# Subtracting the row maximum of two groups of local attention scores inside PSUM, with one exponential for a whole bank

## The chip, the cores and the metric

The program runs on one core of a Trainium2 chip. The metric is the device time of one execution, in microseconds (us). Before the change the median of three runs is 656.81 us, with 656.26 the lowest and 657.3 the highest. A core has a matrix engine (TensorE, PE in the profile), a vector engine (VectorE, DVE), an activation engine (ScalarE, ACT), GpSimd (POOL) and SyncE (SP), which issues the DMAs here. TensorE writes its results to PSUM; everything else lies in SBUF.

## The reference, cut to what matters

The input is q, k and v of 4 batches, 8 heads, 576 positions and 64 features. Each batch goes through an attention with two parts, whose outputs are added:

```
out_d     = softmax attention over q, k, v averaged over groups of 4 positions, repeated 4 times
scores    = q @ k.T / 8, with -1e9 where |i - j| >= 4
scores    = scores - max(scores, axis=-1)
attn      = exp(scores);  attn = attn / (sum(attn) + 1e-9)
out_local = attn @ v
x         = out_d + out_local
```

Then a mixer follows (Fourier transforms over positions and features, their real part added to x, a layer norm, a feed-forward layer of 512 to 2048 to 512), and a gated layer with a short causal convolution and two products of 512 by 512. The change concerns the local attention, and only that of batch 0.

## The kernel before

The local scores are made in windows: 58 query positions see 64 key positions. Two windows make a pair on the 128 partitions, and the five pairs form three groups: pair 0, pairs 1 and 2, pairs 3 and 4. For a group of two pairs the scores of 4 heads stand in one PSUM bank of 128 x 512 (2 pairs x 4 heads x 64 keys), and those of the other 4 heads in another. In the code `par` is the bank, `z` the pair and `a` the head in it.

Batch 0 has steps of its own, in `chain0`; the other batches use `attn_steps`. For each group g of batch 0 there are these steps: `S` (`score`, L1612 and L1622) puts the mask into the bank with a product of identity and band and adds the products of q and k; `M` (`score_max`, L1635) takes the maximum of each row of 64 on VectorE; `X` (`score_exp`, L1640 and L1645) multiplies the maxima by -1/8 and takes the exponential, one ScalarE instruction for each pair and head, since the maximum goes in as a bias of one number a partition, and each gives its row sum through ScalarE's accumulator; `N` (`score_norm`) divides; `T` (`turn`, L1659) transposes on TensorE; `V` (`value`, L1671 and L1683) multiplies with v, on top of the coarse attention's output `base`; `B` (`value_add`, L1693) copies into `X`.

The coarse attention runs beside it for four pairs of heads a: `s` scores (L1705), `m` maxima (L1712), `x` exponentials (L1721), `n` diagonal of reciprocals, `t` (L1738) and `v` (L1747). `q` and `k` pool positions for it (L1697), and `p` pools v on TensorE (L1761). Meanwhile `w` steps decode the eight blocks of the first weight matrix on VectorE, in three passes each (the first at L618, the others at L519), and further steps decode the second matrix. When X is complete, VectorE folds it (`f`, L1790), ScalarE and VectorE split it into two 16-bit parts (`h`, `l`), TensorE mirrors it (`R`, L1826 and L1827) and makes the Fourier products (`e`, L1816; then `Q`, `I`), VectorE adds the results back, and `O` (L1900) centres the input of the first of 12 units of 192 positions. From there a main stage runs, nearly all of it matrix products (the first are L1280).

The order on every engine is written out by hand: `ORDER` lists for each engine the steps by number, with the instructions of a step after a point (so "46.2" is instruction 2 of step 46). In the numbering 19, 26 and 35 are `S0`, `S1`, `S2`; 20, 30, 41 the maxima; 24, 36, 46 are `X0`, `X1`, `X2`; 32, 52, 70 `N0` to `N2`; 107 is the first fold and 163 the centring `O`. Of the decoding 79 is the third pass of block 3, 143 that of block 4, 129 that of block 5, 84 the first pass of block 7; 131 converts the convolution weights; 167 to 169 decode blocks of the second matrix. Step 0 has the memset of `ones`, step 185 the windows of v for batch 1, 183 the scale of W1, 195 a pooling of batch 1.

Of the kernel before, what the change touches and what calls it, by code (L numbers as in the profile page):

```python
# [9 lines left out]
F32 = mybir.dt.float32  # L10
# [3 lines left out]
AF = mybir.ActivationFunctionType  # L14
ALU = mybir.AluOpType
# [13 lines left out]
SCALE = 0.125  # L29
# [25 lines left out]
0 2 1 4 3 5.1 5.0 11 13 7 6 14 16.0 9 8 195.1 10 16.1 12 15.0-1 15.4 15.2 199 195.0 15.3 122 123.0 119.2 201 15.5  # L55
123.1 16.2 119.3 200 119.0 185.0 202 119.1 170 204 203 172.0 206 171 172.1 205 173 174 219.1 185.1 219.0 185.2 237.1
237.0 238.1 238.0 317.1 292 293 296.1 296.0 270 316.1 297 279 316.0 317.0 367.1 318.0 332 367.0 318.1 368.0 318.2
368.1 378.2 378.0 349 378.1 369.1 369.0 370.0 353 370.1 387.0 378.4 378.3 387.1-2 488.1 436.1 394.0-2 387.3-4 397.0-2
398.1 394.4 435.1 386 398.0 394.3 398.2 402.0-2 397.3-4 488.0 418 435.0 409.0-1 402.3-4 409.2 436.0 437.0 415.1 415.0
415.2 409.3-4 415.3 422.0-1 415.4 422.2-4 494.1 494.0 437.1 475 491.0 437.2 462 491.1 505.0 492 505.1 493 520 530 540  # L60
583.1 551 528.1 528.0 503 583.0 562.0 528.2 563 562.1 548 544 569 576.1 576.0 591 598.1 598.0 581 605.0 613.0 605.1
613.1 621.1 621.0 628 635 643.1 643.0 611 622 651 657.1 657.0 672.0 665.1 665.0 672.1 679 641 680 670 684.1 684.0 703
706 707
""",
    "gpsimd": """
5.0 0.0 5.1 136 195.1 0.1 139 137.1 137.0 195.0 294.0 183.0-1 183.3 183.2 193 219.1 219.0 225.0 237.1 225.1-2 121
195.2 237.0 237.2 225.3 219.2 238.1 238.0 238.2 267.1 267.0 275 277 282 280 283.1 283.0 285.0 294.1-3 291.0-1 294.4
291.2-6 298.0 291.7-8 298.1-2 286.1 298.3 286.0 285.1 347.0-1 326 347.2-3 333 367.1 367.0 345 367.2 368.0-1 369.1
# [21 lines left out]
344.1 347.1 333.2 345.1 355.2 355.0 355.3 355.1 356.3 333.3 359.3 356.0 462.1-2 347.2 356.1 388 356.2 359.0 347.3-6  # L90
# [297 lines left out]
S_K = -11.75  # L388
# [1734 lines left out]
```

## Time and profile before

| what | value |
|---|---|
| median of 3 runs | 656.81 us (656.26 to 657.3) |
| the profiled execution's own time | 656.03 us |
| its span, first to last instruction | 654.2 us |
| instructions in the span | 20464 |
| mean granted TensorE clock | 0.991 of full |

The profile is of one execution, so sums of its instructions are to be set against 656.03 us; 1.8 us of that lie outside the span. The median of the runs is 0.8 us above it. A busy TensorE in this profile is not TensorE at its peak: matmuls are pipelined, their ends are modelled, and the granted clock can be half. Idle time of an engine is listed with what ended it.

### The profile page before, as it was taken

Reading aid. Unit: us, or ns where it says so; the run is one execution under the profiler, and the core shown is the slowest. Engines: PE = TensorE matmul, PEld = TensorE weight load, DVE = VectorE, ACT = ScalarE, POOL = GpSimd, SP = SyncE. Lnnn points to the kernel's source line nnn. Section 1 sums busy time; section 2 is a strip of 40 time slices with the busy share of each in tenths; the row PEclk is TensorE's granted clock in tenths of the full one; section 3 lists DMA queues with packets and bytes.
Section 4 is the critical chain, followed back from the end, with each engine's and each line's share of the span. In section 5 each row is a group of like instructions: output and inputs, shape, how many; then the busy total and the mean of one; then the engine's idle time right before and its main releaser. Section 6 shows DMA issues by size and latency. Waiting matters only on the chain.

```text
span 654.2 us, 20464 instructions
## 1 busy us (share of the span) xinstructions
PE 644.7 (99%) x8658; PEld 576.2 (88%) x8659; DVE 524.6 (80%) x1142; ACT 357.2 (55%) x1057; POOL 109.8 (17%) x162
## 2 busy tenths in 40 slices
PE   9999999999999999999999999999999999999997
PEld 4768899999998897998998888997899989998995
DVE  3899899899897978688999858996878868686564
ACT  2787577888535666777454788544232333314223
POOL 0000131420211802710311154031100200200000
PEclk9969999999999999999999999999999999999999
DMA  9995493222343011344363372263424233225301
GB/s 295 416 360 145 166 324 134 74 75 98 103 141 117 18 59 44 111 130 115 121 208 123 101 246 99 78 220 100 151 94 152 98 130 117 112 67 184 123 3 49
DMA packets 44302, 89.98 MB, mean 138 GB/s; under 512 B 3391, under 2 KB 24895, under 8 KB 43186
## 3 DMA queue, kind: packets, MB, share of 16 engines
q1 hardware_dynamic: 44210, 88.67, 40.6%
q8 instruction: 68, 1.11, 0.7%
q14 instruction: 24, 0.20, 0.1%
HBM read 73.77 MB, written 16.65 MB: 138 GB/s over the span
## 4 chain that ended last, share of the span: by engine, by line
PE 93%; DVE 3%; ACT 2%; POOL 1%; issue 0%; DVEq 0%; POOLq 0%
PE pc L1386 25%; PE ph L1316 12%; PE ph L1337 8%; PE out L1507 7%; PE val L1491 6%; PE p L1337 6%; PE pc L1291 3%; PE ph L1280 3%; PE ab L1067 1%; PE dO L876 1%; PE po L1761 1%; PE po L1601 1%; PE sc L954 1%; PE po L999 1%; PE st L1151 1%; PE pq L1090 1%
## 5 line engine op out<-in xcount | busy, mean ns | idle before, releaser
L1386 PE MATMUL pc<-hh,W 128*128 128x192 f16 x1232 | 170.2, 246 | 0.0
L1386 PEld LDWEIGHTS <-W 128*128 128x128 f16 x1848 | 152.4, 98 | 4.5 <-issue 2.8
L1386 PE MATMUL pc<-hl,W 128*128 128x192 f16 x616 | 129.5, 246 | 0.0
L1316 PE MATMUL ph<-u,W 128*128 128x192 f16 x960 | 94.3, 246 | 0.7 <-ACT u L1196 0.4
L1316 PEld LDWEIGHTS <-W 128*128 128x128 f16 x960 | 80.1, 98 | 3.0 <-issue 0.9
L1337 PEld LDWEIGHTS <-W 128*128 128x128 f16 x1632 | 77.9, 98 | 2.2 <-issue 0.2
L519 DVE SCALAR_TENSOR_TENSOR W<-X,cw,W 128x192 f32<-128x192 f32 x160 | 63.2, 427 | 0.4 <-ACT W L1454 0.2
L1337 PE MATMUL ph<-u,W 128*128 128x96 f16 x960 | 62.8, 206 | 0.0
L1349 ACT ACTIVATE hh<-r 128x384 f16<-128x384 f32 x48 | 23.7, 517 | 70.8 <-DVE r L525 60.0
L1491 PE MATMUL val<-yy,W 128*128 128x192 f16 x576 | 58.2, 246 | 0.2 <-DVE W L519 0.2
L1491 PEld LDWEIGHTS <-W 128*128 128x128 f16 x576 | 47.6, 98 | 2.4 <-issue 1.2
L1337 PE MATMUL p<-u,W 128*128 128x96 f16 x672 | 48.0, 206 | 0.0
L1507 PE MATMUL out<-W,gh 128*128 128x512 f16 x144 | 46.0, 379 | 0.0
L525 DVE TENSOR_TENSOR r<-ph,r 128x384 f32<-128x384 f32 (+1 forms) x48 | 21.8, 455 | 26.3 <-PE ph L1337 21.1
L840 ACT ACTIVATE dP<-dS,dmx 128x64 f32<-128x64 f32 x120 | 36.2, 331 | 1.5 <-PE dPT L859 1.2
L525 DVE TENSOR_TENSOR r<-p,r 128x192 f32<-128x192 f32 (+1 forms) x72 | 27.7, 418 | 6.5 <-PE p L1337 4.9
L519 DVE SCALAR_TENSOR_TENSOR hl<-r,hh 128x384 f16<-128x384 f32 x48 | 26.7, 576 | 7.8 <-ACT hh L1349 7.7
L1320 ACT ACTIVATE hh<-ph 128x384 f16<-128x384 f32 x40 | 19.4, 487 | 20.7 <-PE ph L1316 17.3
L519 DVE SCALAR_TENSOR_TENSOR W<-W,W 128x1024 int32<-128x1024 int32 x24 | 29.3, 1230 | 0.1
L1507 PE MATMUL out<-W,gl 128*128 128x512 f16 x72 | 27.3, 379 | 0.0
L519 DVE SCALAR_TENSOR_TENSOR hl<-ph,hh 128x384 f16<-128x384 f32 x40 | 21.8, 551 | 6.8 <-ACT hh L1320 3.8
L840 ACT ACTIVATION_READ_ACCUMULATOR dP<-dS,dmx 128x1 f32 x120 | 27.0, 225 | 0.0
(308 smaller groups left out, 1429.7 us busy)
## 6 DMA issues: line engine op xcount, KB each, us to landing
W<-sums SPq DMA_DIRECT2D x32, 512.0 KB
W<-in_moe_w_ch_dram SPq DMA_DIRECT2D x12, 1024.0 KB
sm<-sums SPq DMA_DIRECT2D x16, 512.0 KB
out_dram<-osb SPq DMA_DIRECT2D x17, 256.0 KB
vw<-in_vw_dram SPq DMA_DIRECT2D x8, 512.0 KB
w1f<-W SPq DMA_DIRECT2D x8, 512.0 KB
sums<-so SPq DMA_DIRECT2D x16, 256.0 KB
v<-in_vp_dram SPq DMA_DIRECT2D x24, 144.0 KB
```

The lines of the kernel that those rows point to most:

```text
L519: return eng.scalar_tensor_tensor(out=out, in0=in0, scalar=scalar, in1=in1, op0=op0, op1=op1)
L525: return eng.tensor_tensor(out=out, in0=a, in1=b, op=ALU.add)
L840: A.activation(out=s_[:, z, a], in_=pss[par][:, z, a], func=AF.Exp, scale=SCALE, bias=mx[:, par, z, a:a + 1], accum_out=su[:, par, z, a:a ...
L1280: T.matmul(out=ps[:, e], lhsT=W[AT[kc * 2 + m // 8] + 1][:, o:o + 128], rhs=u()[:, kc, :], start=(kc == 0), stop=(kc == 3))
L1291: T.matmul(out=c["ps"][m // 2][:, m % 2], lhsT=W[9 + g][:, o:o + 128], rhs=hs[g // 2][:, g % 2, e, :], start=(kk == 0 and m % 2 == 0), sto ...
L1316: T.matmul(out=ps[:, e], lhsT=w1_ap(pw, kc, 2 * g + e), rhs=uh[px][:, kc, :], start=(t == 0), stop=(t == 11))
L1320: A.activation(out=h_, in_=ps, func=AF.Relu)
L1337: T.matmul(out=out[:, e * HT:e * HT + HT], lhsT=w(pw, kc, e), rhs=b_[x](px, kc), start=(kc, pw, px) == (0, 0, 0), stop=(kc, pw, px) == (1, ...
L1349: A.activation(out=h[0], in_=x, func=AF.Relu)
L1386: T.matmul(out=ps[m // 2][:, m % 2], lhsT=w2_ap(pw, kk, m), rhs=x[px][:, e], start=(kk == 0 and (pw, px) == (0, 0) and m % 2 == 0), stop=( ...
L1491: T.matmul(out=ps[:, e], lhsT=wv_ap(pw, kc, 2 * mh + e), rhs=m_["y"][px][:, kc, :], start=(t == 0), stop=(t == 11))
L1507: T.matmul(out=ps, lhsT=(gh, gl)[px][:, kc, t * 128:(t + 1) * 128], rhs=wo_ap(pw, kc), start=(n == 0), stop=(n == 11))
```

## The change

For groups 1 and 2 of batch 0 (`ONE_EXP`) the maxima are multiplied by -1 in place of -1/8. Then TensorE makes the scores a second time into the same banks, mask and products of q and k, and adds a product of the fp32 identity with the negated maxima, each spread over its 64 columns. The bank then holds the scores less their maxima, and one exponential with the scale 1/8 takes all 512 columns. Its row sums are made by VectorE from the result. Group 0 is left as it was, and so are the other batches. The written order is a new one for the first part on every engine, up to about step 245; behind that it is the same.

```diff
+ONE_EXP = (1, 2)
...
-                T.matmul(out=ps, lhsT=eyeb, rhs=m, start=True, stop=False)
                 pss.append(ps)
+            S_["ps", g] = pss
+            score_sum(g, m)
+            S_["m", g] = m
+
+        def score_sum(g, m, neg=None):
+            prs, pss = GROUPS[g], S_["ps", g]
+            n = len(prs)
+            for par in range(2):
+                T.matmul(out=pss[par], lhsT=eyeb, rhs=m, start=True, stop=False)
+                if neg is not None:
+                    T.matmul(out=pss[par], lhsT=eye, rhs=neg[:, par].unsqueeze(3).to_broadcast([P, n, 4, WK]),
+                             start=False, stop=False)
             for z, pr in enumerate(prs):
...
         def score_exp(g):
             n = len(GROUPS[g])
             su[g] = tiny.tile([P, 2, n, 4], F32, tag="dsu", name="dsu")
-            A.activation(out=mx[g], in_=mx[g], func=AF.Copy, scale=-SCALE)
+            A.activation(out=mx[g], in_=mx[g], func=AF.Copy, scale=-1.0 if g in ONE_EXP else -SCALE)
+            if g in ONE_EXP:
+                score_sum(g, S_["m", g], mx[g])
+                for par in range(2):
+                    s_ = S_[g, par] = sp.tile([P, n, 4, WK], F32, tag="S", name="dP", bufs=NS)
+                    A.activation(out=s_, in_=S_["ps", g][par], func=AF.Exp, scale=SCALE)
+                    V.tensor_reduce(out=su[g][:, par], in_=s_, axis=AX.X, op=ALU.add)
+                return
```

The first part of the order, for VectorE up to the centring (step 163), for ScalarE up to the last copy into X (103), and the head of SP's:

```diff
     "sync": """
-0 2 1 4 3 5.1 5.0 11 13 7 6 14 16.0 9 8 195.1 10 16.1 12 15.0-1 15.4 15.2 199 195.0 15.3 122 123.0 119.2 201 15.5
+0 1 2 3 4 5.0 11 14 6 5.1 7 9 13 8 185.0 10 12 15.0 16.1 15.2-5 15.1 195.0 123.0 122.0 201 195.1 16.2 16.0 119.1 123.1
...
     "vector": """
-0 30 20 21 18 32 25 28 41.1 41.0 131.0 48.0 38.0 48.1 38.1 48.2 23 48.3 27 131.1 54.0-1 31 34 54.2 58.0 54.3 65 42 59
-58.1 71.0-1 77.0 71.3 71.2 77.1 86 75 55 85 56 130 63 52.0-1 81.0 52.2-3 132 60 68 73 70.0 83 70.1-2 81.1 70.3 140 67
-81.2 129 81.3-5 107.1 107.0 113.0 109.1 109.0 81.6 110 113.1 114 117 118 79 125 143 84 169.3 169.0 88 136 137 139 133
-145 146 147 150 153 154 156 157 159 165 163 167.0-1 160 192.0-1 167.2 168.0 169.4 168.1 164 168.2 192.2 209 169.1
+30.0 20 30.1 18 21 32.0-1 28 32.3 32.2 23 0 25 41.1 41.0 36 52.0 48.0-2 27 31 48.3 56 38.1 38.0 52.1 52.3 52.2 54.0-1
+42 54.2 58.0 34 60 65.1 65.0 54.3 59 71.0-2 77.1 77.0 71.3 75 58.1 68 86 85.0 55 85.1-3 46 63 67 70.0-1 81.0 70.2 73
+81.1 70.3 81.2 130 83 81.3 84 140 81.5 132 143 81.4 79 107.1 107.0 109.1 109.0 131.0 110 113 114 117.1 117.0 118 129
+125 88 168.0 133 136 137 139 167.0 81.6 167.1 145 146 147 150 169.0 153 154 156 157 159 160 163 165 164 192.0 169.3
...
     "scalar": """
-5.1 24.0 36.0-1 24.1-2 24.5-6 24.3 24.7-8 24.4 37 29.0 29.3 29.1-2 29.4 46.0 62.0 40.0-1 40.3-4 40.2 46.9-10 36.9 36.2
-62.1 66 46.1 106.1 72 46.11 36.10 69.0-1 74 69.2-4 106.0 78 36.3-5 80.0-1 80.3 82 80.4 80.2 36.6 36.11 87 36.7 5.0
-46.12 36.8 36.12-13 89 36.14-16 46.13 90 46.2 46.14 46.3 46.15 46.4 46.16 46.5 93 46.6-7 94 46.8 92 105 175 95 97 98
-100 99 176 102 103 108 112 116 177 124 178 179 134 135 138 180 181 144 182 149 152 183 209 155 184 192.0 192.5 192.1
+5.0 24.0-1 24.5 36.0 24.6-7 24.2-3 24.8 24.4 36.2 36.1 37 5.1 29.0-3 46.0 29.4 62 40 66 69.0 74.0 69.3 72 69.1 69.4
+69.2 74.1 78 80.0-1 80.3 80.2 80.4 82.1 82.0 46.1-2 87 89 106.1 90 175 94 92 95 93 106.0 105 97 98 100 99 102 103 108
+112 176 116 177 124 178 179 180 134 135 138 181 144 182 149 152 155 183 166.0 209 198 166.1 192.0-1 192.5 192.2 184
...
     "tensor": """
-17 26.1 26.0 19.10 19.23 19.1 19.0 19.2-3 19.24-25 19.11-12 19.5 19.26-27 19.4 19.6 19.8 19.7 19.9 19.28 19.13-14
-26.2-3 26.5 26.7 26.4 26.6 26.9 26.8 26.10-23 26.25 26.24 26.27 26.26 26.28 26.30 26.32 26.29 26.31 26.33 19.15 19.17
-19.16 19.18 19.20 19.19 19.21-22 19.29-36 39.0 43.0 44.0 45.0 49.0 50.0 51.0 53.0 22.1 57.0 22.0 22.3 22.2 37 35.1
-35.3 35.0 35.2 35.4-5 35.7 35.6 35.8-9 35.11 35.10 35.12-13 35.15 35.14 35.17 35.16 35.18-27 35.29 35.28 35.31 35.30
-35.33 35.32 39.1 61.0 43.1 33 62.0 44.1 45.1 49.1 50.1 51.1 53.1 64.0 57.1 61.1 64.2 62.1 47.0-8 66.0-1 66.4-6 66.2-3
-66.7 47.9-19 72 64.1 64.3 74.4 74.0 74.5 74.1 74.6 74.2-3 74.7 78 76.0 76.2 76.1 76.3 82.4 82.0 82.5 82.1-3 82.6-7 87
+17 26.0-1 19.0 19.10 19.1 19.23-24 19.3 19.2 19.25 19.11-12 19.5 19.26-27 19.4 19.6 19.28 19.13 19.8 19.7 19.9 19.14
+26.2-5 26.7 26.9 26.6 26.8 26.10-23 26.25 26.24 26.27 26.26 26.28 26.30 26.32 26.29 26.31 26.33 19.15-18 19.20 19.19
+19.21-22 19.29-36 36.2 36.0-1 36.3-28 36.30 36.32 39.0 43.0 22 44.0 45.0 35.0-3 35.5 36.29 36.31 36.34 36.33 36.35
+35.4 35.7 35.9 35.11 35.6 35.8 37 35.10 35.12-13 35.15 35.14 35.17 35.16 35.19 35.18 35.20-22 35.24 35.23 35.25-29
+35.31 35.30 35.33 35.32 49.0 50.0 39.1 43.1 51.0 44.1 53.0 45.1 57.0 49.1 46.0 46.2 33.1 33.0 33.3 33.2 50.1 51.1 61.0
+53.1 57.1 62.0 61.1 62.1 46.3 46.1 46.4-5 47 46.6-14 46.16 46.15 66.0-1 66.4 66.2 66.5-7 66.3 64 72.0-1 74.0-3 72.2-3
+46.17-25 46.27 46.26 46.28-30 78.0 74.4-7 76.1 76.0 76.2-3 46.31 46.33 46.32 46.35 78.1-3 46.34 82.0-1 82.4 82.2-3
+82.5-7 87.0-1 81 87.2-3 89.0-2 89.4 89.3 89.5-7 90 94 95 91.0-3 91.6-7 91.10-11 91.14 91.4-5 91.8 91.15 91.9 91.12-13
```

## Rows read from the trace of the kernel before

**Rows 1.** The page: busy time, share of the span and instructions of each engine.
```profile
PE 644.7 (99%) x8658; PEld 576.2 (88%) x8659; DVE 524.6 (80%) x1142; ACT 357.2 (55%) x1057; POOL 109.8 (17%) x162
```

**Rows 2.** Busy time by engine in three stretches; granted clock, DMA share, GB/s.
```profile
9.88:52.10 42.22, 40.16 (x475) 28.67 (x465) 37.93 (x75) 32.22 (x152) 0.00 (x0) 0.88 1.02 370
...
52.10:74.20 22.10, 21.65 (x213) 17.40 (x213) 19.18 (x38) 14.01 (x29) 2.85 (x14) 1.00 0.49 172
...
74.20:654.20 580.00, 574.04 (x7866) 526.00 (x7867) 467.29 (x1029) 309.34 (x876) 106.42 (x141) 1.00 0.36 117
```

**Rows 3.** Timeline of TensorE: start, us, line, operation; idle before it and its releaser.
```profile
74.25 2.87 PE L1280 MATMUL ph<-u,W 128*128 128x192 f32 x16 [0.46 <-DVE u L1900]
```

**Rows 4.** Timeline of VectorE, instructions on which the sum rests.
```profile
19.06 1.29 DVE L1635 TENSOR_REDUCE dmx<-dS 128x8 f32<-128x512 f32 x2 [0.34 <-PE dS L1622]
...
22.90 0.68 DVE L618 TENSOR_SCALAR W<-X 128x1024 int32<-128x1024 int32 x1
...
42.29 1.29 DVE L618 TENSOR_SCALAR W<-W 128x1024 int32<-128x1024 int32 x2
...
47.59 2.35 DVE L519 SCALAR_TENSOR_TENSOR W<-W,W 128x1024 int32<-128x1024 int32 x2
...
52.10 1.94 DVE L1790 TENSOR_TENSOR fF<-X 128x289 f32<-128x289 f32 x5 [0.66 <-ACT X L1693]
...
73.24 0.95 DVE L1900 TENSOR_TENSOR u<-X,st 128x768 f32<-128x768 f32 x1 [0.71 <-PE st L1896]
```

**Rows 5.** Timeline of ScalarE, the second group's exponentials.
```profile
23.00 0.31 ACT L1645 ACTIVATE dP<-dS,dmx 128x64 f32<-128x64 f32 x1
...
23.28 0.31 ACT L1645 ACTIVATE dP<-dS,dmx 128x64 f32<-128x64 f32 x1
```

**Rows 6.** Groups of ScalarE from 9.88 to 52.1 us: busy, mean ns, idle before.
```profile
L1662 ACT ACTIVATE PT<-dPT 128x512 f32<-128x512 f32 x5 | 2.9, 599 | 2.3 <-PE dPT L1659 2.2
```

**Rows 7.** Timeline of VectorE, waits ahead of the first fold, and a pooling.
```profile
11.75 1.34 DVE L1697 TENSOR_REDUCE qkT<-X 128x288 f32<-128x1152 f32 x1
...
15.01 0.17 DVE L1650 TENSOR_SCALAR dsu<-dsu 128x8 f32<-128x8 f32 x1 [0.66 <-ACT dP L1645]
...
16.64 0.82 DVE L1712 TENSOR_REDUCE nm<-sc 72x2 f32<-72x288 f32 x2 [0.43 <-PE sc L1705]
...
28.16 0.45 DVE L1712 TENSOR_REDUCE nm<-sc 72x2 f32<-72x288 f32 x1 [0.50 <-PE sc L1705]
...
31.05 0.17 DVE L1726 TENSOR_SCALAR lsu<-lsu 72x4 f32<-72x4 f32 x1 [0.39 <-ACT E L1721]
...
39.45 0.18 DVE L1650 TENSOR_SCALAR dsu<-dsu 128x16 f32<-128x16 f32 x1 [0.57 <-ACT dP L1645]
```

**Rows 8.** Timeline of TensorE, from the third group's scores to the mirror products.
```profile
17.02 0.38 PE L1612 MATMUL dS<-bandb 128*128 128x512 bf16 x1
...
17.90 1.10 PE L1622 MATMUL dS<-kTa,X 64*58 64x64 f32 x62
...
20.34 2.75 PE L1761 MATMUL po<-vw,plm 64*72 64x256 f32 x12
...
48.70 1.70 PE L1671 MATMUL dO<-base,eye 128*128 128x456 f32 x4
...
52.12 1.77 PE L1826 MATMUL mir<-X,mirror 128*128 128x289 f32 x6
```

**Rows 9.** Timeline of SyncE's queue, the first block of W1.
```profile
11.00 0.37 SPq L528 DMA_DIRECT2D X<-in_moe_w_ch_dram  x1
```

**Rows 10.** Short stretches as in rows 2, granted clock third from the end.
```profile
32.00:34.00 2.00, 1.25 (x16) 1.14 (x16) 2.00 (x5) 1.89 (x12) 0.00 (x0) 1.00 1.09 421
...
34.00:36.00 2.00, 1.46 (x11) 1.11 (x12) 1.92 (x7) 2.00 (x14) 0.00 (x0) 0.75 0.86 279
...
44.00:46.00 2.00, 2.00 (x7) 0.88 (x6) 1.90 (x3) 1.97 (x6) 0.00 (x0) 0.69 1.06 447
```

**Rows 11.** Timeline of TensorE, its longest wait ahead of the clock's fall.
```profile
34.37 0.71 PE L1747 MATMUL po<-ET,vr 72*64 72x144 f32 x8 [0.93 <-ACT ET L1741]
```

More of the change, by code (lines that the diff above doesn't have):

```diff
@@ new lines @@
+621.1 621.0 628 635 643.1 643.0 611 622 651 657.1 657.0 672.0 665.1 665.0 672.1 679 641 680 670 684.1 684.0 703 706
+707
+""",
+    "gpsimd": """
+5.1 5.0 0.0 136.1 136.0 137.1 137.0 139.1 139.0 183.0-2 195.1 195.0 193 219.0-1 225.0 0.1 183.3 237.1 225.1 294.0
+225.2 121 195.2 237.0 237.2 225.3 219.2 238.1 238.0 238.2 267.1 267.0 275 277 282 280 283.1 283.0 285.0 294.1-3
+291.0-1 294.4 291.2-6 298.0 291.7-8 298.1-2 286.1 298.3 286.0 285.1 347.0-1 326 347.2-3 333 367.1 367.0 345 367.2
+368.0-1 369.1 369.0 369.2 403.0 315 368.2 403.1 433 370.1 370.0 370.2 403.2-3 408 412 419.1 419.0 424 423 427.0 444.1
@@ new lines @@
+299.4 304.3 407.1 283.1 309 297.0 306.3 297.3-4 297.1 285 407.2 297.5 297.2 286 291.0-1 338 291.2 342 407.4 291.3
+294.0 291.4 326.1 326.0 294.1-2 322 313.0 350.1 291.5 339 291.6 326.2 311.0 350.0 298.1 354 298.2 311.1 319 333.0-1
+328.2 357 313.1 298.0 332 364 326.3 328.1 328.3 328.0 329.1 331.1 329.3 329.0 329.2 331.2 331.0 371 331.3 334.1-3
+334.0 341.0 379 347.0 324 344.0 345.0 341.1 344.1 347.1 333.2 345.1 355.2 355.0 355.3 355.1 356.3 333.3 359.3 356.0
+462.1-2 347.2 356.1 388 356.2 359.0 347.3-6 361.0 359.1 347.7-9 361.3 345.2-3 359.2 395 376.3 366 347.10 400 407.3
@@ new lines @@
+629.4 670.2 626.0 623.1 626.1 637.0-2 633.1 633.0 637.5 639.0 637.3 637.6 637.4 650 639.1 638.1 638.3 638.2 639.2
+645.0-1 642.1 645.2-3 645.5 645.4 645.6 639.3-4 644.1 642.3 638.0 644.3 639.5-7 653.0-1 642.2 639.8 644.2 653.2-3
+653.5 646.3 642.0 653.6 653.4 639.9-13 644.0 658.0 646.1-2 658.1-2 658.5-6 646.0 658.3-4 639.14 652.0 639.15 662.1
+655.0 652.1 667.0 655.1 667.1 662.0 667.2-3 667.5 667.4 667.6 668.0 671.0 664 668.2 674.0-3 674.5 668.3 671.2-3 673.3
+674.4 673.2 668.1 674.6 671.1 681.0-3 675.2 673.0 681.5-6 675.3 675.0 681.4 673.1 685.0-2 685.5 685.3 685.6 675.1
@@ L63 @@
+666.3 666.2 667.2 674.0 680 670 664 674.1-2 681 685.0 685.2 677 685.1 690 691 699 701 693 703 700 704 702.1 702.0 705
 706 707
 """,
[L65 to L68, printed above, removed]
@@ new lines @@
+127.5-6 127.12 127.7-9 127.13-15 127.10-11 127.16-22 127.25-27 127.23 127.28-35 126.0 126.3 126.1 141.0-5 142.0
+142.9-10 142.1 142.11-12 142.2 142.13 142.3-8 142.14-17 141.6-8 148.0-6 148.9 148.7-8 148.10-17 151 128.1 183 158
+192.1 161 162 192.0 192.2-10 192.12 192.14 192.11 192.13 192.16 192.15 192.17 193.0 191.0-2 166 193.1-3 184.0-1 191.3
+184.2-7 191.4-7 194.0-5 226.2 226.0-1 193.4-7 197.1 196.0 197.0 194.6-7 196.1-7 197.2-27 197.29 197.28 197.30-31
+197.33 197.32 221.0-1 208 226.3-4 226.6 226.5 226.7 215 231.2 231.0 231.3 231.1 231.6 231.4-5 231.7 218.0-3 235.2
@@ new lines @@
+252.3 252.6-7 269.7-10 265.13-23 249.1 249.0 249.3 249.2 244.8-9 244.12 244.10-11 244.14-15 244.18 244.13 244.16-17
+244.19 244.22-23 244.20-21 244.24-36 244.38-39 244.37 269.11 274.0-11 264.6 264.0 264.7-8 264.1-2 264.9-10 264.3
+269.12-15 274.12-13 264.4-5 264.12 248.4 248.0 248.5 248.1-2 274.14-16 248.6-7 248.3 274.17-19 269.16-17 264.13-14
+264.11 264.15 264.18-20 264.16-17 264.21-23 253.0 248.8-11 269.18-23 274.20-23 268.6 268.0 268.7 268.1 268.8 268.2
+268.9 268.3-4 268.10-11 268.5 268.18-20 268.12-14 268.21 268.15-17 268.22-23 272.6 272.0 272.7-8 272.1 272.9-11
```

194 lines of the change are left out of this document (84 added, 110 removed).

## The prediction

> **What bounds the kernel now.** I read the page first. TensorE is busy 99% of the span, VectorE 80% [rows 1]. An average of that kind says nothing about a change in the start, so next I cut the span at two events: 52.10, where VectorE first folds the finished attention output of batch 0, and 74.2, where it has centred the first unit's input [rows 2]. The reader is to see three different stages.
>
> From 74.2 on TensorE is busy 574.04 of 580 us. I take this block as fixed: its queue order is unchanged from about step 245 on, and the same matmuls stand ahead of that. It begins when the centred input is there: the first product of unit 0 at 74.25 waits 0.46 us for VectorE's `u` [rows 3]. So the price of this change is the shift of that one subtraction, which starts at 73.24 [rows 4].
>
> From 9.88 to 52.10 VectorE is busy 37.93 of 42.22 us, ScalarE 32.22, and TensorE 40.16 at a mean clock of 0.88. At full clock TensorE would get back some 12% of 42.22, 5.1 us; with its 2.06 us of idle time it has 7.1 us of cover. VectorE has 4.29 us, and in the next stage, to 74.2, another 22.10 - 19.18 = 2.92. VectorE is thus the tightest engine, and the new reductions go to it.
>
> **The change part by part.** *ScalarE* loses 32 exponentials of 64 columns. They start 0.28 us apart, accumulator reads included [rows 5], so 32 x 0.28 = 9.0 us go. Four exponentials of 512 columns come. No row shows one; the nearest is the copy of 512 PSUM columns, 0.60 us [rows 6], and from above twice that. I take 0.65, so 2.6 come and 6.4 us are saved net. ScalarE was busy 76% of the stage and VectorE 90%, so this saving shortens the stage only as far as VectorE can follow.
>
> The trace also bears on a rule of the Trainium skill, Perfetto Trace Analysis, section Identifying the Most-Contended Engine: find the engine with the highest occupancy in the regime and relieve that one first. By that rule this change works the wrong way round in this stage, and by it alone the time would rise by the reductions put on VectorE, the 2.6 us of the next paragraph; the ledger below comes to 2.0 by other terms.
>
> *VectorE* gets four sums of 128x512. The same shape as a maximum is a pair in 1.29 us [rows 4], so four are 2.6. The new order also moves weight decoding: ahead of the first fold now stand the third pass of w3 and of w4 and the first pass of w7, behind it the third pass of w5. Third passes are a pair in 2.35, first passes a pair in 1.29 [rows 4]: net 1.18 + 0.65 = 1.8. Two small conversions of the convolution weights leave and a memset of `ones` comes: -0.2 together, by the shortest rows of this engine. Ahead of the fold VectorE therefore has 2.6 + 1.8 - 0.2 = 4.2 us more to do, against 4.29 us of idle time.
>
> How much idle time the new order leaves is the main unknown. From below it is none: the fold then starts 4.29 - 4.2 = 0.1 us early. From above it is as much as now: 4.2 late. I place it by the waits. Two of the old ones go: the first normalisation (0.66) now stands behind a pooling, and the second (0.57) no longer waits for 16 exponentials [rows 7]. The waits of the coarse attention chain stay (0.50 and 0.39 in rows 7), since its four heads still run maximum, exponential, diagonal, product one after another; with the maximum of head 0 now behind two more poolings I count 1.5 for them. One is new: the maximum of the third group's scores waits until those scores are made, and TensorE makes them behind the second set of the second group. VectorE comes to it at about 19.1: the poolings begin at 11.75 as now, four at 1.34, and the first normalisation with the coarse maxima takes what it takes now from 15.01 to 17.46 less a wait of 0.43, 2.0 [rows 7]. On TensorE those scores ended at 19.0; they come 3.3 us later for the second set (next paragraph) and 2.3 earlier because five pooled-value products were put behind them (12 entries, two to a product, take 2.75) [rows 8], so at 20.0. With the passing on of the result I take a wait of 1.0. Idle time 2.5, then. The fold starts at +4.2 + 2.5 - 4.3 = +2.4 us.
>
> *TensorE* gets a second set for each of two groups: two mask products (0.38 at most each), 32 score products, which are 64 entries (62 in 1.10 us), and two fp32 products of the identity with the negated maximum spread over 512 columns. Nothing in the trace has that last shape, but the base products of 456 columns do: four entries, two products, in 1.70 [rows 8]. That makes 0.5 to 0.7 + 1.1 + 1.7, 3.3 us a group, 6.6 in all, hidden as long as the 7.1 us of cover are there. One fp32 mirror product (two of six entries in 1.77, rows 8, so 0.4 without the tail) is moved from ahead of the first Fourier product to behind the last, where TensorE waits anyhow: -0.4 us between fold and centring.
>
> *Between fold and centring* VectorE gets the third pass of w5 and three passes of W2 instead of the two of w3 and w4, the first of w7 and one half pass: +0.3 us, which I cost at nothing, since 2.92 us are idle there.
>
> *Queues.* SP now issues a value window of batch 1 (256 KB) ahead of the first weight block, issued at 11.00 before [rows 9] and first read at 22.90 without a wait [rows 4]; 11.9 us cover it. The other weight blocks are issued ahead of the store that SP used to sit behind, so earlier. On POOL the scale of W1 goes ahead of the pooling of batch 1; neither is on the chain. If these covers fail, the loss is under 1 us.
>
> **Sum.** Centring shifts by +2.4 - 0.4 = +2.0. The profiled execution took 656.03 us on its own time, for a span of 654.2; it gives 658.0. The median of the runs is 0.8 above that execution, so I forecast 658.8.
>
> **The rivals.** *TensorE becomes the bound.* The granted clock was full (2.4 GHz) from 32 to 34, averaged 0.75 over the next two us, and 0.69 from 44 to 46, where it came back [rows 10]; between lay half clock, 1.2 GHz. From 32 to 34 TensorE was busy 1.25 of 2.00 us, and its longest gap ahead of the fall was 0.93 [rows 10, 11]. The new order keeps that coarse tail, so it can fall again, and then the 5.1 us of cover do not exist: 6.6 against 2.06, the fold +4.5, the centring +4.1, in all 660.9. Against it: the second set fills TensorE just there.
>
> The Trainium skill, TensorE: Matmul & The Clock Gate, section Why this matters for your kernels, puts the fall down to one long idle gap between bursts of matmuls. The trace disagrees, with gaps of 0.93 us at most ahead of it. By that rule the clock would stay up in the new order, and this rival would not come about at all.
>
> *No measurable change.* If VectorE's idle time is 1.0 in place of 2.5, the fold is at +0.9 and the centring at +0.5: 657.3. For it: the waits on ScalarE are shorter throughout. The same outcome follows if the shift is there and the six idle microseconds of TensorE after 74.2 take it up.
>
> *Faster: VectorE runs through.* With ScalarE relieved VectorE finds every input ready. Then the fold is at -0.1, the mirror product gives 0.4, and of the 2.92 us behind the fold 1.7 go: centring -2.2, 654.6. It decides once the idle time ahead of the fold is under 1 us and that behind it under 2. Against it: the gaps behind the fold are waits for products and copies that this change leaves alone.
>
> *The change does not relieve ScalarE*, because a 512-column exponential costs twice the copy: +2.2 us on ScalarE, still 4 below before, so no other time.
>
> **Numbers.** The chances are 0.40 for the forecast (all of it slower), 0.20 for TensorE as the bound, 0.27 for no measurable change, 0.13 for faster. A shift of 0.2%, 1.3 us, is about what a measurement of this kernel can tell from none. So slower 0.60, same 0.27, faster 0.13. The range goes from 655.8, most of the way to the faster case, to 662.0, past the second one by the 1.1 us by which its sum can be short. The forecast's own range is 658.1 to 660.2.
>
> **What would show it.** In the profile after: ScalarE's busy time down by some 6 us net of table reads (more in the records, where accumulator reads overlap), VectorE's up by 2.6; in the first stage the four sums at 0.65 each and the identity products at 0.4 an entry; the maximum of group 2 waiting about 1 us; the first fold at 54 to 55; the centring at 75 to 76; a stage of 580 us behind it. A fold before 53, a stage behind it that is shorter than 21 us, or a clock that stays full and lets VectorE run through, makes the forecast wrong on the low side; a fold past 56 with a half clock makes it wrong on the high side.

## The result, and the profile after

The changed kernel takes 659.88 us (median of 5 runs, 659.73 to 661.95) against 656.81 for the kernel before (655.72 to 657.3); the ratio is 1.0056, with a 95% interval of 1.0039 to 1.0074. The forecast of 658.8 was 1.1 us short, and the direction was right. The profiled execution took 659.73 us on its own time, for a span of 657.8.

The page of the changed kernel, its line of engines:

```profile
PE 649.7 (99%) x8799; PEld 578.7 (88%) x8799; DVE 525.6 (80%) x1146; ACT 349.0 (53%) x997; POOL 107.7 (16%) x162
```

Against [rows 1] ScalarE has 8.2 us less to do and VectorE 1.0 more over the span: the page says little here, as it did before. The stages say more. The next rows cut the span of the changed kernel at the first maximum on VectorE (10.10; 9.88 before), the first fold and the centring; columns as in [rows 2].

```profile
10.10:57.28 47.18, 45.83 (x616) 31.69 (x605) 41.62 (x80) 23.73 (x90) 0.00 (x0) 0.93 0.78 287
57.28:77.53 20.25, 20.24 (x182) 16.35 (x182) 18.64 (x38) 14.56 (x31) 1.88 (x10) 1.00 0.68 263
77.53:657.80 580.27, 574.70 (x7900) 526.52 (x7899) 465.37 (x1029) 309.25 (x875) 105.19 (x146) 1.00 0.36 118
```

The first stage was 42.22 us [rows 2] and is 47.18 now: +4.96. From the fold (52.10) to the centring (73.24) it was 21.14 [rows 4]: now 20.25, -0.89. The rest was 654.2 - 73.24 = 580.96: now 580.27, -0.69. With the first maximum 0.22 later that makes +3.60, the difference of the two spans. So the first stage costs more than the whole change, and a part comes back behind it. Every length "of the first stage" below runs from the first maximum to the first fold, so that the moment at which the first loads land (9.88 to 11.48 in these profiles) drops out.

Timeline of TensorE in the changed kernel, one second set and the end of the stage:

```profile
12.10 0.59 PE L1623 MATMUL dS<-bandb 128*128 128x512 bf16 x2
12.58 1.98 PE L1625 MATMUL dS<-dmx,eye 128*128 128x512 f32 x4
14.49 1.10 PE L1635 MATMUL dS<-kTa,X 64*58 64x64 f32 x54
...
40.24 0.47 PE L1766 MATMUL po<-ET,vr 72*64 72x144 f32 x4 [1.21 <-ACT ET L1760]
...
55.49 1.68 PE L1702 MATMUL dO<-PT,vw 64*64 64x58 f32 x64
```

Between the gap of 1.21 us and the last local value product, which ends at 57.17, TensorE has no idle time that the timeline shows. Timeline of VectorE in the same execution:

```profile
16.09 1.35 DVE L1716 TENSOR_REDUCE qkT<-kTa 128x288 f32<-128x1152 f32 x1 [1.21 <-DMA kTa<-in_k_dram]
...
20.64 1.29 DVE L1647 TENSOR_REDUCE dmx<-dS 128x8 f32<-128x512 f32 x2 [0.46 <-PE dS L1635]
21.85 1.27 DVE L1658 TENSOR_REDUCE dsu<-dP 128x8 f32<-128x512 f32 x2
...
57.28 1.57 DVE L1809 TENSOR_TENSOR fF<-X 128x289 f32<-128x289 f32 x4 [1.67 <-ACT X L1712]
...
77.53 0.95 DVE L1919 TENSOR_TENSOR u<-X,st 128x768 f32<-128x768 f32 x1 [0.32 <-PE st L1915]
```

VectorE reaches the fold and then waits 1.67 us for a copy on ScalarE. ScalarE's timeline shows what that copy waits for, and one pair of the new exponentials:

```profile
19.03 1.08 ACT L1657 ACTIVATE dP<-dS 128x512 f32<-128x512 f32 x2 [4.73 <-PE dS L1635]
...
56.68 1.08 ACT L1712 ACTIVATE X<-dO 128x456 f32<-128x456 f32 x2 [1.55 <-PE dO L1702]
```

It is TensorE's last value product, so at the end of the stage VectorE and ScalarE are the engines that wait. That already speaks against the forecast's ledger, in which VectorE set the fold. In the kernel before it was no different: the fold's own line in [rows 4] has VectorE waiting 0.66 us for that copy, and TensorE's last value product and the copy stand there as

```profile
50.32 1.68 PE L1683 MATMUL dO<-PT,vw 64*64 64x58 f32 x64
```

```profile
51.52 1.08 ACT L1693 ACTIVATE X<-dO 128x456 f32<-128x456 f32 x2 [0.79 <-PE dO L1683]
```

The granted clock (third from the end) in the changed kernel's short stretches:

```profile
38.00:40.00 2.00, 1.03 (x16) 0.88 (x14) 2.00 (x4) 1.97 (x11) 0.00 (x0) 1.00 0.11 18
40.00:42.00 2.00, 1.73 (x16) 1.25 (x17) 1.97 (x7) 1.45 (x4) 0.00 (x0) 0.93 0.93 277
42.00:44.00 2.00, 2.00 (x16) 1.53 (x15) 2.00 (x4) 0.89 (x3) 0.00 (x0) 0.50 0.91 200
...
48.00:50.00 2.00, 2.00 (x38) 1.37 (x38) 2.00 (x3) 0.65 (x2) 0.00 (x0) 0.86 0.47 114
```

It still falls from 2.4 to 1.2 GHz, later than in [rows 10] and for a shorter time: half clock from about 41.7 to 48.6 us, where before it was from about 35.0 to 45.2.

### The profile page after: what moved, and what is told of

Its sections match the earlier page's. It is cut to its first block, busy times and chain, and to the rows that moved or that the text cites. A ratio compares the mean times of both kernels' runs of the same rounds, so it can differ in the third digit from the quotient of the medians.

```text
span 657.8 us, 20679 instructions
## 1 busy us (share of the span) xinstructions
PE 649.7 (99%) x8799; PEld 578.7 (88%) x8799; DVE 525.6 (80%) x1146; ACT 349.0 (53%) x997; POOL 107.7 (16%) x162
```

## The experiments

Two theories stood against each other. **V**, the forecast: VectorE's work and waits set the first fold. **T**, its second case: TensorE's added work sets it, less what idle time and clock take up. T's ledger from the rows above, taking half clock as half of the time lost: TensorE's busy time at full clock was 40.16 - 0.12 x 42.22 = 35.1 us and is 45.83 - 0.07 x 47.18 = 42.5, so +7.4; idle time 2.06 to 1.35, -0.7; time lost to half clock 5.1 to 3.3, -1.8. The sum is the +4.96, but it comes out so by construction, and the half is an estimate on the high side (run 4). A sum that need not come out is this one: two masks, the fp32 products and 54 of the 64 score entries of a second set take from 12.10 to 15.52, so a whole set takes some 3.6 us and two take 7.2; less 0.7 of idle time, and less what 3.4 us less of half clock give back, 1.1 to 1.7 at a third to a half, that makes 4.8 to 5.4. Each ratio below is to the kernel before, run beside it on the same chip.

**1. No sums.** VectorE without the four sums:

```diff
-V.tensor_reduce(out=su[g][:, par], in_=s_, axis=AX.X, op=ALU.add)
+V.tensor_scalar(out=su[g][:, par], in0=s_[:, :, :, 0], scalar1=0.0, scalar2=1.0, op0=ALU.mult, op1=ALU.add)
```

> Left out: the four sums of 128x512 on VectorE; in their place VectorE writes ones (four instructions of 128x8), so the probabilities stay unnormalised. Everything else, queue orders too, is as in the changed kernel. Theory V (VectorE's ledger sets the first fold, as forecast): VectorE loses 4 x 0.64 and gets back about 4 x 0.15, so the fold goes from 57.28 to about 55.2 and the median falls by about 2 us, to 657.9. Theory T (TensorE's unbroken run from 40.24 to 57.17 us sets it): the fold moves by less than 0.6 us and the median stays between 659.2 and 660.2.

Measured: 661.03 us, ratio 1.0066 (1.0046 to 1.0087). First stage (columns as above), and the fold on VectorE's timeline:

```profile
10.60:57.76 47.16, 45.80 (x617) 31.65 (x606) 39.58 (x81) 23.66 (x90) 0.00 (x0) 0.93 0.77 285
```

```profile
57.76 1.57 DVE L1809 TENSOR_TENSOR fF<-X 128x289 f32<-128x289 f32 x4 [2.67 <-ACT X L1712]
```

VectorE is busy 39.58 us in place of 41.62, and the stage is 47.16 in place of 47.18. The last wait took half of the 2.04 us that went (1.67 to 2.67), earlier waits the rest. V falls. The median is 3.15 us above the kernel before beside it (657.88); counted from 656.81, T had 2.4 to 3.4 and V 1.1.

**2. Negated maxima in bfloat16.** TensorE with less work, VectorE with the same:

```diff
+neg = tiny.tile([P, 2, n, 4], BF16, tag="dnb", name="dnb") if g in ONE_EXP else mx[g]
-A.activation(out=mx[g], in_=mx[g], func=AF.Copy, scale=-1.0 if g in ONE_EXP else -SCALE)
+A.activation(out=neg, in_=mx[g], func=AF.Copy, scale=-1.0 if g in ONE_EXP else -SCALE)
...
-T.matmul(out=pss[par], lhsT=eye, rhs=neg[:, par].unsqueeze(3).to_broadcast([P, n, 4, WK]),
+T.matmul(out=pss[par], lhsT=eyeb, rhs=neg[:, par].unsqueeze(3).to_broadcast([P, n, 4, WK]),
```

> The negated maximum is rounded to bfloat16 and added by a bfloat16 identity; the sums are taken of the same exponentials, so the result stays a softmax. The four entries of 128x512 that now take 1.98 us a group should take about 0.6, like the two mask products of the same width. Theory T: TensorE gets 2 x 1.4 = 2.8 us less to do, so the fold comes 1.5 to 3 us earlier and the median falls to 657 to 658.5. Theory V: VectorE's work is the same, the fold moves by less than 0.6 us, 659.3 to 660.3.

Measured: 660.40 us, ratio 1.0045 (1.0028 to 1.0062). TensorE's negated maxima, and the first stage:

```profile
13.32 0.59 PE L1625 MATMUL dS<-dnb,bandb 128*128 128x512 bf16 x2
```

```profile
10.83:56.03 45.20, 42.95 (x613) 30.77 (x601) 41.40 (x80) 23.73 (x90) 0.00 (x0) 0.92 0.80 292
```

1.98 us became 0.59 in each group, 2.8 together; TensorE's busy time fell by 2.88, 0.90 of it turned into idle time, and the stage is 1.98 us shorter. T, and in the stage inside its bounds. The median shows less of it (2.5 us above the kernel before, where T had 0.2 to 1.7): the block behind the centring is 581.42 in this execution, 1.15 longer.

**3. The negated maxima twice.** The dose the other way: each maximum halved and added twice.

```diff
-A.activation(out=mx[g], in_=mx[g], func=AF.Copy, scale=-1.0 if g in ONE_EXP else -SCALE)
+A.activation(out=mx[g], in_=mx[g], func=AF.Copy, scale=-0.5 if g in ONE_EXP else -SCALE)
...
-if neg is not None:
+for _ in range(0 if neg is None else 2):
```

> The changed kernel with each negated maximum halved and added twice: four more identity products of 512 fp32 columns on TensorE, 1.98 us a group by the profile of the changed kernel, 4.0 in all; the result is the same, VectorE and ScalarE have the same work. Theory T: from the first maximum to the fold 47.2 becomes 50.2 to 52.2 (more or less by how long the clock stays down), the median 3 to 5 us above that of the changed kernel, so 6 to 8.5 above the kernel before. Theory V: no more than 0.6 us above the changed kernel.

Measured: 665.11 us, ratio 1.0108 (1.0090 to 1.0125). TensorE's products and the first stage:

```profile
12.98 3.70 PE L1625 MATMUL dS<-dmx,eye 128*128 128x512 f32 x8
```

```profile
10.49:61.11 50.62, 49.25 (x625) 33.17 (x613) 41.74 (x81) 23.78 (x90) 0.00 (x0) 0.93 0.71 262
```

3.70 - 1.98 = 1.72 us more a group, 3.44 in all, and the stage is 50.62 - 47.18 = 3.44 longer. VectorE's work is the same. What TensorE gets to do here is paid one for one, as T had it; the median, 7.56 us above the kernel before beside it, is inside T's bounds as well.

**4. The changed kernel again**, on the chip of the next three.

> The changed kernel itself, once more, on the chip of the next three, so that they can be compared with it. Both theories: 2 to 4 us above the kernel before; from the first maximum on VectorE to the first fold 47.2 us as in its first profile, if that length is the kernel's and not the run's.

Measured: 661.68 us, ratio 1.0065 (1.0046 to 1.0084). First stage:

```profile
11.48:59.78 48.30, 46.96 (x616) 32.52 (x605) 41.45 (x80) 23.78 (x90) 0.00 (x0) 0.89 0.75 277
```

48.30 and not 47.2: the length is not the kernel's alone. The same 616 records of products on the same queues ran at a mean clock of 0.89 in place of 0.93; the half clock lasted 10.2 us here, from 41.1 to 51.4, and 6.8 in the first profile. Those 3.4 us more cost TensorE 1.1 us more of busy time (46.96 for 45.83, at the same idle time), a third and not the half of the ledger. The median is 4.4 us above the kernel before, where both theories had 2 to 4. So single stages compare to about a microsecond unless their clocks agree, as they do in runs 1 and 3.

**5 to 7. Form and order apart.** Run 5 keeps the new orders and goes back to 32 exponentials (the new steps' entries taken out of the orders):

```diff
-ONE_EXP = (1, 2)
+ONE_EXP = ()
```

> The new queue orders with the old form of the exponentials: no second set on TensorE, no sums on VectorE, 32 exponentials of 64 columns on ScalarE in place of four of 512. TensorE loses about 7.5 us of work in the first stage, VectorE 2.6, ScalarE gets 6.4 more. Theory T: the second sets are what costs, the fold is back at 51 to 54 and the median at 655.5 to 657.5. A rival O, that the new order is what costs whatever the form: the median stays at 659 or above. Theory V lies between: 2.6 us less, about 657.3.

Runs 6 and 7 put the new form into the old orders, with f32 and with bfloat16 maxima:

```diff
 # tensor: the second sets (36 second group, 46 third group)
-35.32 39.1
+35.32 36 39.1
...
-47.0-8 66.0-1
+47.0-8 46 66.0-1
...
 # scalar: two exponentials where one of the old ones stood, the others taken out
-36.9
+36.1-2
...
-46.11
+46.1-2
...
 # vector: the sums
-54.3 65
+54.3 36 65
...
-77.1 86
+77.1 46 86
```

> The new form of the exponentials in the queue orders of the kernel before, with only the new instructions put in: second set of the second group ahead of the pooled-value products' second half, of the third group ahead of the Gram product; exponentials and sums where ScalarE and VectorE had the group's work. Theory T (TensorE's added work is what costs): from the first maximum to the fold 42.2 us before, plus 7.5 of work less what idle time (2.1) and clock (5.1) take up, so 43 to 47, and the median 0 to 4 us above the kernel before. Theory O (the new order is what costs): no more than 0.5 us above the kernel before.

> As the run before, with the negated maxima in bfloat16. Theory T: TensorE's added work falls from 7.5 to 4.6 us, so the fold comes 1.5 to 3 us earlier than in the run before and the median is within 1.5 us of the kernel before, on either side. Theory O: the same time as the run before it, within 0.6.

Measured: run 5 668.80 us, ratio 1.0173 (1.0140 to 1.0207); run 6 665.46, 1.0117 (1.0099 to 1.0135); run 7 663.06, 1.0088 (1.0073 to 1.0102). First stages of runs 5, 6 and 7:

```profile
10.66:61.69 51.03, 44.67 (x477) 31.17 (x466) 39.40 (x77) 31.28 (x150) 0.00 (x0) 0.77 0.77 281
```

```profile
10.37:61.72 51.35, 48.93 (x616) 34.13 (x605) 40.00 (x79) 25.23 (x92) 0.00 (x0) 0.83 0.84 303
```

```profile
11.02:58.47 47.45, 45.16 (x611) 32.43 (x601) 39.95 (x79) 25.07 (x92) 0.00 (x0) 0.86 0.89 324
```

T's numbers failed for runs 5 and 6, by 4 us and more. Run 5 by itself came out as O had it. In it the exponentials stand in two blocks of 16 on ScalarE, the second in the coarse tail: there TensorE waits 2.00 us for a copy of `base` behind them, it idles 6.4 us in the stage, and the clock averages 0.77. So the new orders do not suit the old form. In run 6 TensorE has the 616 records of the changed kernel, but gaps of the old order stay (the longest 0.99 us), and half clock lasts some 17 us (0.17 x 51.35, doubled). The ledger puts TensorE's work at full clock at 48.93 - 0.17 x 51.35 = 40.2 us here, at 42.5 in the changed kernel and at 41.6 in run 4, for the same products: its terms are good to two microseconds and no better. In the old orders the form costs 9.1 us in the stage, and the new orders win 3.1 to 4.2 of them back (51.35 to 48.30 in run 4 and 47.18 in the first profile): for the new form O is wrong in sign. Run 7's stage is 3.9 shorter than run 6's, and TensorE's busy time 3.8; its median is still 5.8 us above the kernel before, where T had expected 1.5 at most; its clock is at half for more than 13 us, longer than T had counted, but no run shows that this is all of it.

**8 to 10. Holding the clock.** Dummy products on TensorE at the gap ahead of the third coarse value product. In run 8 they write the bank of that product, and 0.91 us of the gap stay ahead of them; in run 9 they write a bank that is free since the second group's exponentials; run 10 is run 9 with bfloat16 maxima and one load of K issued ahead of a value window. Run 9's edit:

```diff
+for _ in range(16 if g == 0 else 0):
+    T.matmul(out=pos[0].rearrange("p a n -> p (a n)")[:, 0:P], lhsT=busy, rhs=busy, start=True, stop=True)
...
 # tensor (and the later entries of step 91 counted on by 16)
-82.5-7 87.0-1 81 87.2-3
+82.5-7 91.0-15 87.0-1 81 87.2-3
```

> 18 dummy products of 128x128 f16 are put on TensorE ahead of the third coarse value product, where it stood idle for 1.21 us (39.03 to 40.24) just ahead of the fall of its clock. Theory T: if that gap is what brings the clock down, the granted clock stays full from 40 to 50 us; about 6.5 us at half clock are then 3.2 us saved on TensorE, but VectorE had work ahead of the fold until 55.55, so the fold comes at 54.1 to 55.7 and the median at 657 to 658.5. Theory V: clock full or not, the fold moves by less than 0.6 us. If the gap is not the cause of the fall, the clock still falls and nothing moves under either.

> The changed kernel with 16 dummy products of 128x128 f16 in the gap ahead of the third coarse value product, written to the free bank of the second group's scores, so that they wait for nothing and delay nothing. Theory T: the clock is down for 0 to 3.5 us in place of 6.6, TensorE gets 1.5 to 3.3 us back; VectorE's queue ahead of the fold ends 45.4 us after the first maximum, so that length goes from 47.2 to between 45.3 and 46.2, the centring comes as much earlier, and the median lies 0.8 to 2.5 us above the kernel before. Rival L (what TensorE wins here is lost in the main block, whose order was fitted to the later start): the length shrinks the same, but the block after the centring grows from 580.3 to 582 or more and the median stays 3 us or more above the kernel before.

> As the run before it, with the negated maxima in bfloat16 and the one load of K issued ahead of a value window; no pass of weight decoding is moved. Theory T: from the first maximum to the fold 43.6 to 44.8 us, as in the run with the moved passes (44.15), since TensorE set it there; then 20.3 to the centring, and the median 0 to 1.8 us above the kernel before. Rival L: the block after the centring grows by as much as the start shrinks, and the median stays 2 us or more above the kernel before.

Measured: run 8 662.33 us, ratio 1.0077 (1.0056 to 1.0099); run 9 662.23, 1.0065 (1.0039 to 1.0091); run 10 660.34, 1.0035 (1.0017 to 1.0053). The first stage of run 8, all three stages of run 9, all three of run 10:

```profile
11.03:56.50 45.47, 44.15 (x634) 30.37 (x623) 41.45 (x80) 23.72 (x90) 0.00 (x0) 1.00 0.77 288
```

```profile
10.35:55.86 45.51, 43.96 (x634) 30.16 (x622) 41.46 (x81) 23.75 (x90) 0.00 (x0) 1.00 0.78 290
55.86:76.66 20.80, 20.40 (x181) 16.34 (x181) 18.63 (x38) 14.55 (x31) 1.42 (x10) 1.00 0.69 259
76.66:657.30 580.64, 574.62 (x7899) 526.51 (x7899) 465.42 (x1029) 309.24 (x875) 105.61 (x146) 1.00 0.37 118
```

```profile
9.94:54.83 44.89, 41.46 (x628) 29.13 (x617) 41.50 (x80) 24.09 (x92) 0.00 (x0) 1.00 0.80 299
54.83:76.60 21.77, 20.45 (x181) 16.42 (x181) 18.64 (x38) 14.55 (x31) 1.42 (x10) 1.00 0.66 248
76.60:658.20 581.60, 574.93 (x7899) 526.51 (x7899) 465.73 (x1029) 309.20 (x875) 105.29 (x146) 1.00 0.37 118
```

In all three profiled executions the clock stayed full. The stage shrinks by 1.7 us in runs 8 and 9, as T had it (the fold of run 8 stands later than 55.7 only because its first maximum does). And there it stops: the fold on VectorE's timelines of runs 8 and 10 carries no wait.

```profile
55.31 1.21 DVE L521 SCALAR_TENSOR_TENSOR W<-W,W 128x1024 int32<-128x1024 int32 x1
56.50 1.57 DVE L1811 TENSOR_TENSOR fF<-X 128x289 f32<-128x289 f32 x4
```

```profile
53.64 1.22 DVE L521 SCALAR_TENSOR_TENSOR W<-W,W 128x1024 int32<-128x1024 int32 x1
54.83 1.57 DVE L1812 TENSOR_TENSOR fF<-X 128x289 f32<-128x289 f32 x4
```

VectorE comes to it straight from the last decoding pass. Run 10 takes another 2.5 us of busy time off TensorE (43.96 to 41.46) and gains 0.6 (45.51 to 44.89), which leaves the stage 0.1 above T's bounds. The gain is not the load of K: run 9 does not wait for it, and run 10 waits 0.60 us in spite of its edit. Some of it lies at the third group's maximum, which waits for TensorE in both (1.80 us in run 9, 0.87 in run 10) and comes 10.56 us after the first maximum in run 9, 10.34 in run 10:

```profile
20.91 1.29 DVE L1647 TENSOR_REDUCE dmx<-dS 128x8 f32<-128x512 f32 x2 [1.80 <-PE dS L1635]
```

```profile
15.32 1.35 DVE L1719 TENSOR_REDUCE qkT<-kTa 128x288 f32<-128x1152 f32 x1 [0.60 <-DMA kTa<-in_k_dram]
...
20.28 1.29 DVE L1647 TENSOR_REDUCE dmx<-dS 128x8 f32<-128x512 f32 x2 [0.87 <-PE dS L1635]
```

So VectorE is the next bound, 1.7 us behind TensorE, but not by its decoding passes alone. In runs 9 and 10 TensorE waits 0.98 us for VectorE's last normalised scores, and from there both engines' chains end together. Run 10's TensorE and ScalarE:

```profile
47.26 0.33 PE L1679 MATMUL dPT<-eye,dP 128*128 128x128 f32 x1 [0.98 <-DVE p2a L572]
```

```profile
54.23 1.08 ACT L1715 ACTIVATE X<-dO 128x456 f32<-128x456 f32 x2 [1.55 <-PE dO L1705]
```

The copies begin 0.60 us ahead of the fold (54.83), as they do in the changed kernel (56.68 and 57.28), where the fold waits for them. With fewer decoding passes between the normalisation and the fold, the fold would not have come earlier. Behind the fold the win shrinks again: from fold to centring run 10 takes 21.77 us, where T had 20.3, and VectorE waits there for a weight block:

```profile
69.73 0.69 DVE L620 TENSOR_SCALAR W<-W 128x1024 int32<-128x1024 int32 x1 [1.83 <-DMA W<-in_moe_w_ch_dram]
```

Its load is one of those that SyncE issues from 54.88 on, having waited for VectorE's last decoding pass ahead of the fold. Run 9 waits 0.86 us for it, run 8 0.55, the changed kernel not at all, and from this pass on to the centring runs 8 to 10 take 6.9 us each: behind the fold the load is their bound.

The medians follow only in part. Run 10 is the fastest form of the change, and still slower than the kernel before, by 1.7 to 5.3 thousandths. T's medians were too low for all three (657 to 658.5 for run 8; for runs 9 and 10, 0.8 to 2.5 and 0 to 1.8 us above the kernel before, measured 3.8 and 2.0). Run 9's median is no better than the changed kernel's in run 4 (1.0065 both), although its stage is 1.7 us shorter than in the first profile and 2.8 shorter than in run 4: its profiled execution took 659.13 us, the lowest of its seven (to 664.52). Nor did the dummies keep the clock up each time: its mean was 1.000 in 2 of the 6 executions of run 8, 3 of 7 of run 9 and 6 of 12 of run 10, else 0.992 to 0.999. Rival L is not seen in run 9's block behind the centring (580.64); but run 10's is 581.60, 1.33 longer than the changed kernel's, where the centring comes 0.93 earlier, and run 8's is 582.81. So L is not ruled out.

**11. TensorE and VectorE relieved.** Run 10 with the third passes of w3, w4 and w6 moved behind the fold, and one W2 pass from there to behind the centring:

```diff
 # vector
-84 140 81.5 132 143 81.4 79 107.1
+84 140 81.5 81.4 107.1
...
-118 129 125 88 168.0 133
+118 79 129 125 143 88 132 133
...
-163 165
+163 168.0 165
...
 # scalar: the sum of squares that needs w5 behind the spectrum's copies
-179 180 134 135 138 181
+179 134 135 138 180 181
```

> The changed kernel with what theory T says it costs taken back, and then VectorE relieved: negated maxima in bfloat16; 16 dummy products of 128x128 f16, into the free bank of the second group's scores, in the gap ahead of the third coarse value product, so that the clock stays up; the third passes of w3, w4 and w6 and one first pass of W2 behind the fold; one load of K ahead of a value window, for the 1.21 us that VectorE waited at 16.09. Theory T: TensorE's stage at full clock is then 45.2 less 3.6 (its half-clock loss) = 41.6 us, VectorE's 41.4 less 3.6 of moved passes = 37.8 busy and 3 to 4 idle, so from the first maximum to the fold 41.2 to 42.8, as long as in the kernel before, and the median -0.8 to +1.5 us of the kernel before. If instead the new form or its order has a cost beyond TensorE's work and clock and VectorE's queue, the stage stays above 43.5 and the median 2 us or more above the kernel before.

Measured: 667.61 us, ratio 1.0147 (1.0124 to 1.0169). Two stages, and what VectorE waits for in the second:

```profile
10.07:54.22 44.15, 42.66 (x630) 30.51 (x618) 38.00 (x78) 23.74 (x90) 0.00 (x0) 0.96 0.80 302
54.22:84.46 30.24, 23.00 (x182) 17.73 (x182) 21.35 (x40) 14.65 (x31) 1.20 (x10) 0.89 0.48 179
```

```profile
76.00 0.69 DVE L620 TENSOR_SCALAR W<-W 128x1024 int32<-128x1024 int32 x1 [6.75 <-DMA W<-in_moe_w_ch_dram]
```

A miss by 10 us that teaches a price. The passes that were moved give back the buffer into which the next weight block is loaded; moved behind the fold, they moved that load too (SyncE's queue waited 19.4 us for VectorE's pass, and issued its loads from 60.87 on in place of 54.88), and VectorE stood 6.75 us at its first pass, ahead of the inverse transform that the centring needs. The first stage still answers the question: with VectorE at 38.00 us the fold waits 3.75 us for TensorE's chain, and the stage is 44.15, above the 42.8 that T allowed, with the clock down for some 3 us in spite of the same dummies.

**12. Dummies in the kernel before**, 8 ahead of the second and 18 ahead of the third coarse value product, written to those products' own bank as in run 8.

> The kernel before with dummy products on TensorE ahead of the second (8) and the third (18) coarse value product, at the gaps of 0.39 and 0.93 us. If dummy work there keeps the clock up in this kernel too, up to 5 us at half clock come back to TensorE. Theory T for the kernel before: the fold then comes 2 to 4 us earlier. Theory V for the kernel before (VectorE busy 37.93 of 42.22 sets the fold, as the forecast had it): the fold moves by less than 1 us. If the clock falls all the same, the dummies' 1.5 us are added or hidden and nothing follows.

Measured: 660.04 us, ratio 1.0028 (1.0010 to 1.0046). Its first stage:

```profile
10.50:55.82 45.32, 42.93 (x502) 31.19 (x493) 37.91 (x76) 32.36 (x152) 0.00 (x0) 0.85 0.95 347
```

The profiled execution was at half clock for 13.7 us, longer than the kernel before (0.85 on average), and its stage is 3.1 us longer. The twelve timed runs fall into two groups: four with a mean clock of 1.000 over the span took 656.39 to 657.12 us, eight with 0.986 to 0.990 took 659.76 to 661.35. The two groups lie 2.6 to 5.0 us apart. With the clock up all the time this kernel is not clearly faster than the kernel before, whose median beside it was 657.24 (655.53 to 659.03); that VectorE then sets the fold, at 37.91 us busy, fits but was not profiled. In the profiled execution it does not: the fold waits 1.39 us for ScalarE's copy.

## Why the prediction was right, and where it was not

**The number.** 658.8 was inside its interval by a sum whose main step was wrong. The forecast had the fold at +2.4; it is at +5.2. The mechanism was that of its second case, TensorE as the bound, given 0.20 and 660.9 us: fold +4.5, centring +4.1; measured +5.2 and 77.53 - 73.24 = +4.3. A time in the range did not tell the two apart; runs 1 to 3 did. By the forecast's own sign, a fold past 56 with a half clock, it was wrong on the high side. That the sum landed 1.1 us away is in part luck: the fold came 2.8 us later than forecast, but 0.5 us more came back behind the fold, 0.7 behind the centring, and the median lies 0.15 above the profiled execution where the forecast had added 0.8.

**The step that failed** is the one that hid TensorE's 6.6 us "as long as the 7.1 us of cover are there". The work was nearly right, some 7.2 to 7.4. The cover was not there: of the 2.06 us of idle time 0.7 was used, and of the half clock, which went from 10.2 to 6.8 us, 1.1 to 1.7. Nor was the half clock worth 5.1 in the first place: an estimate by run 4's third makes it 3.4 us, and one by run 9, whose products take 3.0 us less without half clock than the changed kernel's with 6.8 us of it (the dummies' 1.1 us taken off), 4.5. The forecast kept the coarse tail, in which the clock had fallen, and yet counted on getting the clock back. It also passed over the 0.66 us in [rows 4]: VectorE, which it took for the tightest engine, was already waiting for TensorE's chain at the fold, so every microsecond put on TensorE past the cover came on top. The Trainium skill, Perfetto Trace Analysis, section Identifying the Most-Contended Engine, warns against reading TensorE's headroom off its matmul busy share, and would judge it by the share of weight loads, among others. The trace does not agree here: the weight loads were busy 28.67 of 42.22 us [rows 2], 68%, and the products 95%, and it was the 95% that told how little room there was.

**VectorE's terms.** The sums were right (1.27 a pair; 1.29 forecast), the work +3.7 in place of +4.2, the new wait at the third group's maximum 0.46 in place of 1.0. One wait was not foreseen: 1.21 us for the second half of K, which has not landed when its pooling comes up. It cost nothing: in run 4 K is there in time, the third group's maximum waits 1.80 us instead and comes 10.55 us after the first one, as it does in the first profile (10.54). TensorE sets that moment, too. The ledger was in the main a sound account of the wrong engine: 1.7 us behind the one that decided, as runs 8 to 10 show.

**TensorE's terms.** The second set's fp32 products were estimated at 1.7 us from the base products and take 1.98. The base products have 456 columns, and the forecast did not scale them to 512, which gives 1.91. In bfloat16 they take 0.59, 2.8 us less in two groups; the forecast did not look for a cheaper form.

**ScalarE.** Two exponentials of 512 columns take 1.08 us, 0.54 each (0.65 taken). Busy time in the stage falls from 32.22 to 23.73 us, and the stage grows all the same.

**Behind the fold** -0.89 came back in place of -0.4, and another -0.69 behind the centring, which the forecast named as a possibility and did not count. The block there differs by 2.5 us between profiles, so one pair of them does not show that the change has won it.

**The clock.** The second rival's condition, that the coarse tail stays and the clock falls again, came true: a gap of 1.21 us, then half clock 1.5 us after its end (in run 4 within the gap of 1.22). The Trainium skill, TensorE: Matmul & The Clock Gate, section Why this matters for your kernels, puts such falls down to one long idle gap. Runs 8 to 10 show that this place matters: with the gap filled, or followed by dummies, the clock stayed full in the profiled executions. Run 11, with the same dummies as run 10 and a gap of 0.32 left, fell all the same, so the gap's length alone does not settle it.

**What stays open.** Times of one kernel differ by 3 us and more at equal clocks: the kernel before took 655.5 to 659.0 us with a mean clock of 0.988 to 0.992 in each of the 17 runs beside runs 4, 6, 7 and 12. Profiles show two sources, the moment of the first maximum (9.88 to 11.48) and the block behind the centring (580.3 to 582.8); why the block is longer in some executions, and whether an earlier start makes it so, was not settled. Nor is it shown why the clock falls in one execution and not in the next.

## What to carry to other kernels

Before work is given to an engine because it is "covered", ask whether the cover is idle time or a slow clock: here the clock came back fully only in executions with dummies at the gap ahead of its fall, and not in all of those. Look also at the instruction with which the stage ends: what it waits for in the kernel before ([rows 4], 0.66 us) names the engine that has no room. Where two engines are within a few per cent of each other, put a dose on each alone (half the work, double the work) and see which one moves the end; a forecast inside its range is no proof of its mechanism. Price a helper product (an identity times a row of maxima) in the cheapest type that the algebra allows: a softmax's shift need not be exact, and bfloat16 took 0.59 us where fp32 took 1.98.

## What the runs showed of the hardware that was not expected

The granted clock is not a property of the kernel: the changed kernel was at half clock for some 6.8 us in one execution and 10.2 in another, 1.1 us apart in the same stage, and one kernel (run 12) ran with the clock up in 4 of 12 executions, 2.6 to 5.0 us faster. A microsecond at half clock did not cost half a microsecond: 3.4 us more of it made TensorE's busy time 1.1 us longer. And dummies do not always help: in the profiled execution of run 12, where the clock fell nonetheless, the stage was 3.1 us longer than before.
